# One tanh over six score banks in 12 of 56 chunks, with the VectorE work and side jobs placed anew

## The chip, the cores and the metric

The kernel runs on one core of a Trainium2 chip. The metric is the device time of one execution in microseconds (us); lower is better. Engines in the profile: PE (TensorE matmul) and PEld (its weight load), DVE (VectorE), ACT (ScalarE), POOL (GpSimd), SP (SyncE).

## The reference

Softcapped attention over 8 batches, 12 heads, 448 tokens and 64 dimensions, then a mixture of experts with soft slots over the 3584 tokens.

```python
scores = scale * np.matmul(q, k.transpose(0, 1, 3, 2))
scores = cap * np.tanh(scores / cap)                    # cap = 30
attn = np.exp(scores - max);  attn /= attn.sum(-1) + 1e-09
x = np.matmul(attn, v)                                  # -> [3584, 768]
logits = x @ phi                                        # 32 slots
d = softmax of logits over tokens;  slot_input = d.T @ x
slot_out[e] = np.maximum(slot_input[e] @ w1[e], 0) @ w2[e]   # 8 experts
out = (softmax of logits over slots) @ slot_out
```

## The kernel before

Attention works on transposed score tiles of 128 keys by 448 queries, one PSUM bank each. Four heads make a quad, each quad two pairs, each pair seven tiles: 336 tiles, sorted by `order` and cut into 56 chunks of six (`CH`). A chunk is two groups of three (`CS`). `qk_chunk(i)` (L309) writes group i into a three-bank buffer `sc` of the pool `psS` (two buffers, six banks); `tanh_chunk(i)` (L323) reads it on ScalarE into half of the SBUF tile `ex` of its chunk (five such tiles in rotation). The exp of a chunk runs in place one turn later (`exp_chunk`, L336), over the tiles that `SHARED` does not give to VectorE. VectorE computes its share (the first one to three tiles of a chunk) in seven integer and half-precision steps, numbered 0 to 6 (`poly_exp`, L560, steps at L566 to L573).

The main loop (L856) sets each engine's order by hand; there is no scheduler. One turn j issues:

- slot '0'; tanh A (`2j`); slot 'm'; tanh B (`2j+1`); slot 'e'; exp of chunk j-1;
- `pv_first` (L611): attention times V, first four tiles of the pair that ends in chunk j-2; slot 'a'; `pv_tail`;
- `qk_chunk(2j+2)`, the first scores of the next chunk; slot 'b';
- `pv_rest` (L628): the remaining three tiles, then `norm` (L595): reciprocal and multiply on VectorE (L598, L601), which frees PV's single PSUM bank for the next pair; then V casts on POOL for a later quad (L287), each followed by a load of V on SP's queue;
- slot 'c'; `qk_chunk(2j+3)`, the second scores; slot 'd'.

In the chunks with j = 6 mod 7 no pair ends, and PV is skipped.

Slots hold jobs put there by `at`: in each slot those marked '<' come first, then the plain ones, then '>'. `POLY` lists, by (turn, slot), which step of which chunk VectorE takes. `WHEN` gives the turn, relative to 7 times the batch, and the slot of the side jobs: transposes of k and q (`k1` to `q3`, L268, each with a VectorE copy at L279), V casts, loads of k and q through POOL's queue (`lk1` to `lq3`, L181), transposes of the attention output (`x0` to `x2`, L646), logits (`lg`), their exp (`ee`), slot sums (`ss`), transposes of E (`et`, L687) and their row sums (`es`, L703). These side jobs share one PSUM bank, so each waits for the copy out of the one before. `FILL` and `spare` are junk matmuls on ones. One weight load of 384 KB is issued by POOL in slot 'b' of most turns.

After the loop the tail (L887 on) finishes the last pairs, the slot sums, the two expert layers and the output.

## Time and profile before

| what | us |
|---|---|
| median of 3 runs (284.36 to 288.99) | 284.4 |
| the profiled execution | 284.53 |
| its span in the trace | 282.8 |
| PE / DVE / ACT / POOL busy | 247.6 / 241.9 / 250.7 / 139.9 |

The attention loop fills the span from about 7 to 237 us; the granted TensorE clock is 1.00 in all stages of it. A row of the page's groups gives the line, engine, operation and tile, then how many, busy us, mean ns of one, and idle time before it. A timeline row gives start, length, line, and in brackets the idle time before it with what ended it. Chunk 10's first tanh starts at 46.75 us, chunk 21's at 90.65, chunk 35's at 148.04, chunk 52's at 217.73.

### The profile page before, as it was taken

How to read it: one execution, taken by the hardware profiler on the slowest of the kernel's cores; microseconds unless marked ns; L12 is line 12 of the kernel's file. 1: busy time of each engine (PE TensorE's matmuls, PEld its weight loads, DVE VectorE, ACT ScalarE, POOL GpSimd, SP SyncE). 2: the span in 40 equal slices, each digit the busy share in tenths (PEclk: the TensorE clock that was granted, in tenths of full speed). 3: DMA queues.
4: the chain of work that ended last, by engine and by line, in shares of the span. 5: the costliest groups of instructions: out<-in, count | busy, mean ns of one | idle time of the engine just before them, and what ended most of it. 6: DMA issues, size and time to landing. Idle time of an engine off the chain costs nothing.

```text
span 282.8 us, 10259 instructions
## 1 busy us (share of the span) xinstructions
PE 247.6 (88%) x4463; PEld 164.7 (58%) x4463; DVE 241.9 (86%) x473; ACT 250.7 (89%) x211; POOL 139.9 (49%) x197
## 2 busy tenths in 40 slices
PE   8897989999999999899988998899989989998710
PEld 7555556655665667566756675667566758643300
DVE  3499999999999999999998999999999996456740
ACT  3999999999999999999999999999999996247720
POOL 7965647673957375828663758274834220200000
PEclk9999999999999999999999999999999999999975
DMA  7999999999999999999999999999999489959995
GB/s 244 261 203 205 207 214 221 231 180 219 228 225 219 219 232 232 216 216 221 227 219 211 224 216 206 217 223 216 228 215 217 106 290 331 408 209 391 412 427 247
DMA packets 58332, 68.08 MB, mean 241 GB/s; under 512 B 4144, under 2 KB 54448, under 8 KB 58288
## 3 DMA queue, kind: packets, MB, share of 16 engines
q0 software_dynamic: 42448, 35.31, 79.7%
q1 hardware_dynamic: 15552, 31.89, 32.0%
q8 instruction: 35, 0.57, 0.7%
q10 hardware_dynamic: 288, 0.23, 0.2%
q14 instruction: 9, 0.07, 0.1%
HBM read 91.72 MB, written 19.27 MB: 393 GB/s over the span
## 4 chain that ended last, share of the span: by engine, by line
DVE 40%; ACT 29%; PE 18%; issue 5%; DMA 2%; POOL 1%; DVEq 0%; ACTq 0%
ACT ex L329 16%; ACT ex L334 12%; DVE xq L601 6%; DVE ex L572 5%; DVE xp L571 4%; DVE xp L569 4%; DVE xf L568 3%; DVE ex L566 3%; DVE ex L573 3%; PE pv L591 3%; DVE qT L279 3%; DVE xT L653 2%; PE sc L320 2%; DVE xp L570 2%; DVE kT L279 2%
## 5 line engine op out<-in xcount | busy, mean ns | idle before, releaser
L329 ACT ACTIVATE ex<-sc 128x1344 f16<-128x1344 f32 (+1 forms) x113 | 154.9, 1546 | 1.2 <-PE sc L320 1.2
L334 ACT ACTIVATE ex<-ex 128x1344 bf16<-128x1344 f16 (+5 forms) x58 | 118.2, 2051 | 0.1
L591 PE MATMUL pv<-vbd,ex 128*128 128x130 bf16 (+1 forms) x1610 | 93.5, 211 | 8.9 <-DVE xq L601 4.1
L591 PEld LDWEIGHTS <-ex 128*128 128x128 bf16 (+1 forms) x1680 | 75.6, 101 | 35.4 <-PE sc L320 7.3
L287 POOL CAST vbd<-vraw 64x896 bf16<-64x896 f32 x46 | 46.7, 1016 | 62.0 <-PE pv L591 33.6
L320 PE MATMUL sc<-qT,kT 64*64 64x448 bf16 x672 | 70.6, 359 | 2.5 <-DVE qT L279 1.2
L601 DVE TENSOR_TENSOR xq<-pv,rec 128x448 bf16<-128x448 f32 x46 | 28.7, 624 | 1.6
L320 PEld LDWEIGHTS <-kT 64*64 64x64 bf16 x672 | 24.0, 105 | 10.1 <-issue 7.6
L569 DVE TENSOR_TENSOR xp<-xf 128x1344 f16<-128x1344 uint16 (+2 forms) x34 | 27.8, 817 | 0.3
L571 DVE TENSOR_TENSOR xp<-xp,xf 128x1344 f16<-128x1344 f16 (+2 forms) x34 | 26.8, 788 | 0.6
L572 DVE TENSOR_TENSOR ex<-ex,xp 128x1344 uint16<-128x1344 uint16 (+2 forms) x34 | 26.7, 787 | 0.2
L116 POOL DMA_DIRECT2D w1b<-in_moe_w_dram x32 | 25.8, 807 | 0.0
L568 DVE TENSOR_SCALAR xf<-ex 128x1344 uint16<-128x1344 uint16 (+2 forms) x34 | 18.3, 538 | 0.5
L184 POOL DMA_DIRECT2D qb<-in_q_dram x22 | 16.4, 744 | 4.2 <-PE qps L277 2.9
L570 DVE TENSOR_SCALAR xp<-xp 128x1344 f16<-128x1344 f16 (+2 forms) x34 | 17.3, 509 | 0.6
L566 DVE TENSOR_SCALAR ex<-ex 128x1344 uint16<-128x1344 f16 (+2 forms) x34 | 17.2, 506 | 0.6 <-ACT ex L329 0.6
L573 DVE TENSOR_SCALAR ex<-ex 128x1344 uint16<-128x1344 uint16 (+2 forms) x34 | 16.9, 497 | 0.3
L279 DVE COPY kT<-kps 128x896 bf16<-128x896 bf16 x23 | 14.1, 615 | 2.9 <-PE kps L274 2.8
L184 POOL DMA_DIRECT2D kb<-in_k_dram x22 | 16.3, 744 | 0.0
L120 POOL DMA_DIRECT2D w2d<-in_moe_w_dram x21 | 15.9, 769 | 0.0
L295 POOL MEMSET vbd<- 64x1 bf16 x22 | 2.8, 125 | 25.6 <-PE pv L591 25.6
L279 DVE COPY qT<-qps 128x896 bf16<-128x896 bf16 x23 | 14.2, 618 | 0.9 <-PE qps L277 0.9
(123 smaller groups left out, 305.7 us busy)
## 6 DMA issues: line engine op xcount, KB each, us to landing
w1b<-in_moe_w_dram POOLq DMA_DIRECT2D x32, 384.0 KB, 8.9
vraw<-in_v_dram SPq DMA_DIRECT2D x44, 224.0 KB, 6.0
w2d<-in_moe_w_dram POOLq DMA_DIRECT2D x21, 384.0 KB, 9.0
w2t<-w2d SPq DMA_DIRECT2D x21, 384.0 KB, 6.4
out_dram<-ob SPq DMA_DIRECT2D x7, 768.0 KB, 7.8
qb<-in_q_dram POOLq DMA_DIRECT2D x22, 224.0 KB, 7.3
kb<-in_k_dram POOLq DMA_DIRECT2D x22, 224.0 KB, 6.5
w2b<-in_moe_w_dram POOLq DMA_DIRECT2D x11, 384.0 KB, 8.0
```

The source lines that it names most:

```text
L184: pool.dma_start(out=t, in_=quad_ap(nm, Q))
L279: dve.tensor_copy(t, ps)
L287: pool.tensor_copy(vbds[Q % 2][r, :, :, c0:c0 + DH], raw[r])
L320: pe.matmul(sc[cs, u, 0:S], qkT["k", Q][r, c, cs], qkT["q", Q][r, :, cs], start=True, stop=True)
L329: act.activation(exs[j][:, half * CS + u0:half * CS + u1, :].bitcast(F16), (own[0] if i == u0 == 0 else sc)[:, u0:u1, 0:S], ACT.Tanh, scal ...
L334: act.activation(exs[j][:, u0:u1, :], exs[j][:, u0:u1, :].bitcast(F16), ACT.Exp, scale=cap)
L568: lambda: dve.tensor_scalar(s, y, STEP - 1, STEP, ALU.bitwise_and, ALU.bitwise_or),
L569: lambda: dve.tensor_tensor(p, s, s.bitcast(F16), op=ALU.mult),
L571: lambda: dve.tensor_tensor(p, p, s, op=ALU.mult),
L572: lambda: dve.tensor_tensor(y, y, p, op=ALU.add),
L591: pe.matmul(out_, exs[j][r, u, q0:q0 + (HP if tail else P)], v_, start=(c == 0 and g == gs[0] < NF), stop=(c == NT - 1), skip_group_check= ...
L601: dve.tensor_tensor(xq[Q][:, h, s0:s1, :], pv[:, 0:s1 - s0, 0:DH], rec.to_broadcast([P, s1 - s0, DH]), op=ALU.mult)
```

## The change

In the chunks of `JOINED` the two tanh become one instruction over all six banks. From chunk 10 to 52 the two `sc` buffers are one tile, the board, taken from a pool that is closed and opened anew at chunk 10 and at 53; in unjoined chunks between, waits are set by half of the board. In a joined turn the first scores of the next chunk are issued behind slot 'b' and the rest of PV. `SHARED` changes in one entry, chunk 32, from two tiles to three (93 in all). `POLY` is placed anew throughout, `FILL` and `WHEN` in part.

```diff
+    psV = attp.enter_context(tc.tile_pool(name="psV", bufs=1, space=PSUM, side="right"))
+    scp = ExitStack()
+    psS = scp.enter_context(tc.tile_pool(name="psS", bufs=2, space=PSUM))
...
+    def half_of(i):
+        nonlocal psS
+        j, half = divmod(i, CH // CS)
+        if JOINED and half == 0 and j in (JOINED[0], JOINED[-1] + 1):
+            scp.close()
+            psS = scp.enter_context(tc.tile_pool(name=f"psS{j}", bufs=2 - (j == JOINED[0]), space=PSUM,
+                                                 reuse_waits="tile"))
+            if j == JOINED[0]:
+                own["board"] = psS.tile([P, CH, 512], F32, name="sc", tag="board")
+        if JOINED and JOINED[0] <= j <= JOINED[-1]:
+            return own["board"][:, half * CS:half * CS + CS, :]
+        return psS.tile([P, CS, 512], F32, name="sc", tag="sc")
+
+    def own_half(ins, kind, i, behind=None):
+        j, half = divmod(i, CH // CS)
+        other = "qt"[kind == "q"]
+        tc.declare_no_dep(ins, group=f"{other}{1 - half}", reason="other three banks of the score buffer")
+        tc.add_to_no_dep_group(f"{kind}{half}", ins)
+        if behind is not None:
+            tc.add_manual_dep(ins, behind.name, ...)
...
     def tanh_chunk(i):
...
+        if j in JOINED:
+            if half:
+                apart["t", i - 1] = apart["t", i] = act.activation(
+                    exs[j].bitcast(F16), own["board"][:, :, 0:S], ACT.Tanh, scale=qk_scale / cap).ins
+            return
...
+    JOINED = (10, 14, 17, 21, 24, 31, 35, 38, 42, 45, 49, 52)
-    SHARED = {... 32: (2, 0), ...}
+    SHARED = {... 32: (3, 0), ...}
     POLY = {
...
-            (21, 'e'): ((21, 0),),
-            (21, '<a'): ((19, 5), (19, 6)),
+            (21, '<a'): ((19, 5), (21, 0)),
+            (21, '>a'): ((19, 6),),
...
-            (35, '0'): ((33, 6),),
-            (35, '>a'): ((35, 0),),
+            (35, 'e'): ((35, 0), (33, 6)),
...
-            (42, '>a'): ((42, 0), (40, 6)),
+            (42, 'e'): ((42, 0),),
+            (42, '<a'): ((40, 6),),
...
-    FILL = ((7, 'a', fill, 18), (6, 'b', spare, 11), (6, 'c', spare, 3),)
+    FILL = ((7, 'a', fill, 18), (6, 'a', spare, 8),)
...
-    WHEN: 'k1': (-1, 'd'), 'x1': (9, '0'), 'x2': (10, 'a'), 'et': (13, 'e'), 'es': (15, 'c'),
-          'lk1': (-3, 'd'), 'lq1': (0, 'a'), 'lk2': (1, 'c'), 'lq3': (3, 'b')
+    WHEN: 'k1': (0, '0'), 'x1': (8, 'c'), 'x2': (10, 'b'), 'et': (13, 'b'), 'es': (14, 'c'),
+          'lk1': (-2, 'm'), 'lq1': (-1, 'b'), 'lk2': (1, 'd'), 'lq3': (3, '0')
...
-        qk_chunk(2 * j + 2)
+        if j not in JOINED:
+            qk_chunk(2 * j + 2)
         run(j, "b")
...
             run(j, "r")
+        if j in JOINED:
+            qk_chunk(2 * j + 2)
         run(j, "c")
```

## The prediction

> **What bounds the kernel now.** I read the page first (busy time, slices), then the instruction groups with their shapes apart, then the timeline of ScalarE alone, then those of TensorE and VectorE around one chunk. "A" and "B" are the two tanh of a chunk, "first" and "second scores" the two groups of six score matmuls (L320) that chunk j issues for chunk j+1.

> Page, busy time and the slice row of ScalarE:

> ```profile
> PE 247.6 (88%) x4463; PEld 164.7 (58%) x4463; DVE 241.9 (86%) x473; ACT 250.7 (89%) x211; POOL 139.9 (49%) x197
> ...
> ACT  3999999999999999999999999999999996247720
> ```

> Three engines are near 88%, but only ScalarE shows nines from the second slice to the 33rd. The tail after 237 us is untouched by the change. The groups (count, busy us, mean ns):

> ```profile
> L329 ACT ACTIVATE ex<-sc 128x1344 f16<-128x1344 f32 x111 | 153.7, 1561 | 0.0
> L334 ACT ACTIVATE ex<-ex 128x2688 bf16<-128x2688 f16 x21 | 57.1, 2719 | 0.0
> L334 ACT ACTIVATE ex<-ex 128x1344 bf16<-128x1344 f16 x27 | 43.6, 1615 | 0.0
> L334 ACT ACTIVATE ex<-ex 128x1792 bf16<-128x1792 f16 x6 | 11.6, 1934 | 0.0
> ```

> These means hold overlap and are no price. ScalarE's timeline for chunks 20 and 21 (start, us; an "x2" row spans A and B):

> ```profile
> 87.10 2.76 ACT L329 ACTIVATE ex<-sc 128x1344 f16<-128x1344 f32 x2
> 89.44 1.63 ACT L334 ACTIVATE ex<-ex 128x1344 bf16<-128x1344 f16 x1
> 90.65 2.78 ACT L329 ACTIVATE ex<-sc 128x1344 f16<-128x1344 f32 x2
> 92.99 2.77 ACT L334 ACTIVATE ex<-ex 128x2688 bf16<-128x2688 f16 x1
> 95.33 2.80 ACT L329 ACTIVATE ex<-sc 128x1344 f16<-128x1344 f32 x2
> ```

> Ends (start + length) are 89.86, 91.07, 93.43, 95.76, 98.13. So end to end a tanh pair takes 2.36, exp over 1344 takes 1.21, over 2688 takes 2.33. Each starts 0.3 to 0.4 us before its forerunner ends; early on (9.31 + 2.44 = 11.75, next start 11.66) 0.09 was enough. A late start therefore costs nothing until it is later than about 0.1 before the forerunner's end. By this measure ScalarE loses nothing from 16 to 237 us: it is the bound.

> TensorE around the same chunks:

> ```profile
> 88.58 0.49 PE L696 MATMUL eps<-ident,E 128*32 128x128 bf16 x16 [0.45 <-DVE xT L653]
> 89.00 0.56 PE L320 MATMUL sc<-qT,kT 64*64 64x448 bf16 x6
> 89.50 0.66 PE L839 MATMUL junk<-ones 128*128 128x384 bf16 x3
> ...
> 90.33 0.32 PE L839 MATMUL junk<-ones 128*128 128x384 bf16 x1
> 90.58 0.57 PE L320 MATMUL sc<-qT,kT 64*64 64x448 bf16 x6
> ...
> 94.64 0.38 PE L320 MATMUL sc<-qT,kT 64*64 64x448 bf16 x2
> ```

> Second scores for chunk 21 end at 91.15, after A of 21 has started (90.65): today only B needs them. VectorE there, and the hand-over to the tail:

> ```profile
> 92.40 0.50 DVE L566 TENSOR_SCALAR ex<-ex 128x1344 uint16<-128x1344 f16 x1
> 92.81 0.85 DVE L572 TENSOR_TENSOR ex<-ex,xp 128x1344 uint16<-128x1344 uint16 x1
> 93.70 0.51 DVE L573 TENSOR_SCALAR ex<-ex 128x1344 uint16<-128x1344 uint16 x1
> ```

> ```profile
> 231.94 0.34 PE L839 MATMUL junk<-ones 128*128 128x384 bf16 x1 [0.90 <-DVE xq L601]
> ```

> In the chain that ended last ScalarE rules from 80 to 170 us; from 182 to 232 it is VectorE with short TensorE pieces, and TensorE enters the tail after waiting 0.90 for VectorE's norm.

> **The change, part by part.**

> *Twelve joins.* Exp prices: (2.33 - 1.21) / 1344 = 0.833 ns an element, fixed 1.21 - 1.12 = 0.09. A tanh of 1344: 2.36 / 2 - 1.12 = 0.06 fixed. No row shows a tanh over 2688. Low end 0 (PSUM and SBUF reads show one rate, so no loss); high end the unoverlapped start of the first tanh, 0.544 - 448 x 0.833 ns = 0.17. I take 0.06, the row of the same instruction in the same stream: 12 x 0.06 = 0.72 us saved, 0 to 2.0. [...]

> *A third tile of chunk 32 to VectorE.* Exp over 1792 ends 1.59 after its forerunner, over 1344 1.21: 0.37 saved on ScalarE. VectorE pays seven steps of 1344 for seven of 896: 4.74 - 3.78 = 0.96 us. From 140 to 160 us it is busy 18.50 of 20, so 1.5 idle covers it; uncovered, up to 0.96.

> *The joined tanh needs both score groups.* At chunks 14, 21, 42 the second scores came 0.39, 0.50, 0.61 us after A's start; past the overlap that would cost some 0.2 each; at 35 and 49 nothing. The same change moves what stands before them (junk of chunks 6 mod 7: 11 + 3 becomes 8, ahead of the first scores; the E transposes from 'e' to 'b', where they no longer wait 0.45 for the xT copy). B of chunk 20 ends 89.86; without junk in front, second scores run about 89.9 to 90.5, before 90.65. Cost 0, bound 0.7. At 10, 17, 24, 31, 38, 45 they were ready 0.17 to 0.84 before A; at 52 0.58 late, but there x1's transposes (0.75) leave the chunk ahead.

> *First scores now wait for the whole joined tanh (end E) and stand behind side jobs and the rest of PV on TensorE.* At 3 mod 7 the second scores already ran 0.05 after B's end, TensorE being ready; the first scores take that place: E + 0.05 + 0.57 + 0.04 (the shortest score-to-tanh gap shown) = E + 0.66, due at E + 1.21 - 0.1. Free by 0.4. The second scores follow as before. At 21, 35, 42 VectorE's order gets a new wait: step 0 of chunk j, which needs E, stands ahead of the last step of chunk j-2, j-2's last tile is in this PV rest, and the scores queue behind that. Chain: 0.05 + 0.42 (L566) + 0.51 (L573) + 0.43 (94.21 to 94.64) + 0.57 + 0.04 = E + 2.0, due at E + 2.33 - 0.1. It fits by 0.2. Behind step 0 on VectorE also stand that pair's norm and qT copy, and TensorE's next PV waits for the norm. Cost 0.1 in all; bound 0 to 3 x 0.5.

> *The pool is reopened at chunk 10.* The board lies over both old buffers, so the first scores of 10 wait for B of 9 (44.61) in place of A: QK starts 44.66 in place of 43.59. Second scores then end near 46.6, due 46.75. Cost 0.1, bound 1.1. At 53 the wait is for a tanh already waited for: 0.

> *Moved jobs.* Each xT group is 0.75 on TensorE and a 0.6 copy on VectorE: x1 now precedes the second scores of 1 mod 7, which had 0.8 to 1.1 to spare (0.17 at chunk 50, where e_sums' 0.33 leave and the overlap of 0.5 covers). e_sums one chunk earlier ends three waits of at most 0.4 of xps for winv. x2 passes the PV tail only; k1 passes nothing on TensorE. Loads lk1, lq1, lk2, lq3 are POOL issues of 0.74 each: lq1 goes a chunk earlier, ahead of a weight load; lq3 now stands before chunk 3 mod 7's weight load and must wait for q2's transposes just issued, some 0.5, with the V cast behind it; that cast waits for PV's end anyway (33.6 us of such waits). SP's V loads follow the casts. POOL is busy 49%. Cost 0, bound -0.5 to +0.5. Fewer junk matmuls leave TensorE idle, nothing more.

> *Sum.* ScalarE: -0.72 - 0.37 + 0.1 + 0.1 = -0.9. But the tail starts on VectorE's norm, and the chain is VectorE's from 182 on, which idles 0.7, 0.3, 0.2 in the last three stages; what is saved at chunks 45, 49, 52 (0.18) I let lapse. That leaves -0.7 to -0.8. The profiled execution took 284.53 (span 282.8 and 1.7 around it), 0.1 above the median 284.4: 283.7 against it, 283.6 against the median.

> **Rivals.**
> 1. *The full fixed cost is saved.* For: the first tanh alone shows 0.17. Against: the stream shows 0.06. 12 x 0.17 + 0.37 = 2.4: 282.0. [...]
> 2. *Given back.* VectorE, 0.96 us fuller and newly waiting for E, keeps its end at 231; or the joined tanh waits for second scores (0.7). For: it is busy 19.68 of 20 from 200 to 220. Against: 5 us idle before 182. 284.4, up to 285.3.
> 3. *Slower: scores behind PV behind VectorE.* If steps of chunk j-2 come late, the scores do, and ScalarE stops, as it never did. The longest wait of a PV weight load for L573 is 0.6. With 0.1 to 0.4 to spare, a loss of 0.2 to 0.5 in each of 12: +2.4 to +6.0 on 283.6, middle 287. Decides from 0.06 a join (gain gone); 2% from 0.5. Against: second scores sit behind the same PV rest today and arrive.
> 4. *No join in effect* (a start as late as B's): the tile remains, 284.0; part of case 2's range.

> **How the numbers follow.** Forecast 0.50; full fixed cost 0.10; given back, with 4, 0.26; slower 0.14. The forecast with its bounds runs 282.9 to 284.1; reaching to case 1's middle and through case 2 into the low part of case 3 gives 282.2 to 286.2, with under 2 in 10 outside. A change of under 2% (5.7 us) is about what a measurement of this kernel cannot tell from none. Over 2% faster 0.01; only the far end of case 3 is over 2% slower, 0.04; within 0.95.

> **What would show it.** Joined tanh rows ending about 2.30 after their forerunner, 12 of them, against 2.36; ScalarE without idle to 236; exp x1792 down to 5; second scores of chunks 13, 20, 41 ending before the joined start; first scores ending 0.65 after E at 3 mod 7 and about 2.0 at 21, 35, 42. Wrong if joined rows take 2.19 or 2.36, if ScalarE waits for L320, or if TensorE waits more than 0.90 for VectorE near 231.

## The result and the profile after

The changed kernel took 286.86 us (median of 6, 286.20 to 287.67), the kernel before 284.71 beside it on the same chip (6 runs): a ratio of 1.0077, 95% interval 1.0053 to 1.0100. It is slower by some 2.2 us, where 0.8 less than before had been forecast. The profiled execution took 286.76 with a span of 285.0 (before: 284.53 and 282.8). Every ratio here is to executions of the kernel before in the same sitting, whose median went from 284.71 to 285.76 between sittings, so times of different sittings are best compared by their ratios; executions over 1.5% slower than the fastest of their kernel count in the medians, not in the ratios.

The page of the changed kernel: busy time, ScalarE and the granted clock in 40 slices, then three groups.

```profile
PE 247.6 (87%) x4449; PEld 166.2 (58%) x4449; DVE 240.8 (84%) x473; ACT 250.5 (88%) x199; POOL 141.3 (50%) x197
...
ACT  4999988999999999999999999999999997237720
...
PEclk9999979999999999999999999999999999999975
```

```profile
L365 ACT ACTIVATE ex<-sc 128x1344 f16<-128x1344 f32 x87 | 113.6, 1402 | 1.8 <-PE sc L348 1.8
L361 ACT ACTIVATE ex<-sc 128x2688 f16<-128x2688 f32 x12 | 30.6, 2552 | 0.1
L373 ACT ACTIVATE ex<-ex 128x1792 bf16<-128x1792 f16 x5 | 9.1, 1821 | 0.0
```

ScalarE's busy time did not rise. Its row has two new eights, in slices 6 and 7 (36 to 50 us), and the clock row a new 7 in slice 6. By the idle time before them all joined tanh together waited 0.1 us; the unjoined ones 1.8, for scores. That is the prediction's sign of being wrong "if ScalarE waits for L320" (L348 in the changed kernel).

ScalarE's timeline around chunk 21 (start, length); L361 is the joined tanh:

```profile
91.55 1.44 ACT L373 ACTIVATE ex<-ex 128x1344 bf16<-128x1344 f16 x1
92.77 2.52 ACT L361 ACTIVATE ex<-sc 128x2688 f16<-128x2688 f32 x1
95.06 2.56 ACT L373 ACTIVATE ex<-ex 128x2688 bf16<-128x2688 f16 x1
```

The ends are 92.99 and 95.29: 2.30, as forecast. So the saving is there, and something else took more. I measure that as in the prediction: end of a ScalarE instruction less the end of the one before, less its usual length (tanh over 1344 1.18, over 2688 2.30; exp over 1344 1.21, and so on). What is left over is a wait. Before, all such waits from 9 us to the last exp come to 0.27; after, to 3.69:

| after, where | wait, us |
|---|---|
| chunk 8 A, chunk 8 B, chunk 9 B (38.92, 40.65, 45.06) | 0.76, 0.55, 0.84 |
| chunk 10 joined and the tanh behind it (the pool reopened) | 0.16, 0.10 |
| exp of the logits (E, 225.12) | 0.80 |
| others | 0.48 |

From the first tanh (0.41 earlier than before) to the last exp (238.95 against 237.05) the balance is -0.41 for the earlier start, -1.10 saved by the joins and the third tile, and +3.42 for more waits: +1.9. The tail added 0.3.

The largest place is chunks 8 and 9. First the waits over the whole span, after and then before, by sum, count and longest; the row of ScalarE holds one wait at the start in both (0.81 after, 1.22 before):

```profile
ACT ex L365 <- PE sc L348: 2.6, 4, 0.8
PE kps L278 <- DMA kb<-in_k_dram: 2.1, 1, 2.1
```

```profile
ACT ex L329 <- PE sc L320: 1.2, 1, 1.2
PEld L277 <- DMA kb<-in_k_dram: 1.2, 3, 0.5
```

TensorE after, then before, then ScalarE after:

```profile
32.04 0.57 PE L348 MATMUL sc<-qT,kT 64*64 64x448 bf16 x6 [0.36 <-ACT ex L365]
34.68 0.58 PE L278 MATMUL kps<-ident,kb 128*64 128x128 bf16 x14 [2.07 <-DMA kb<-in_k_dram]
...
37.95 0.93 PE L348 MATMUL sc<-qT,kT 64*64 64x448 bf16 x4
```

```profile
32.85 0.56 PE L320 MATMUL sc<-qT,kT 64*64 64x448 bf16 x6
33.48 0.58 PE L277 MATMUL kps<-ident,kb 128*64 128x128 bf16 x14
```

```profile
38.92 1.29 ACT L365 ACTIVATE ex<-sc 128x1344 f16<-128x1344 f32 x1 [0.65 <-PE sc L348]
40.65 1.29 ACT L365 ACTIVATE ex<-sc 128x1344 f16<-128x1344 f32 x1 [0.44 <-PE sc L348]
...
45.06 1.29 ACT L365 ACTIVATE ex<-sc 128x1344 f16<-128x1344 f32 x1 [0.73 <-PE sc L348]
```

The load of k for turn 7's transposes, which the scores of chunk 8 need (`lk3` of batch 0, issued by POOL), landed at 34.64 after and at 33.43 before: there 0.05 us ahead of its use. In the chain of the changed kernel that ended last it stands with its whole flight:

```profile
26.73 7.91 DMA kb<-in_k_dram
```

And the granted clock in three stretches of the changed kernel (length, then busy time of each engine, then the clock, DMA share, GB/s):

```profile
34.00:35.37 1.37, 0.69 (x17) 0.60 (x18) 0.06 (x1) 1.37 (x3) 0.00 (x0) 1.00 1.19 243
35.37:38.78 3.41, 3.24 (x44) 2.23 (x41) 3.34 (x7) 2.90 (x3) 0.00 (x0) 0.50 1.24 218
38.78:42.00 3.22, 2.52 (x48) 1.91 (x47) 2.40 (x6) 2.64 (x3) 1.65 (x2) 1.00 1.08 180
```

Behind the 2.07 us of idle TensorE its clock was halved for 3.41 us, in the very stretch in which the late transposes, PV and scores had to catch up: four score matmuls took 0.93 there (37.95), 0.54 elsewhere. Before, the clock is 1.00 from 6 to 237 us.

### The profile page after: what moved, and what is told of

It is laid out like the page before. It is cut to its first block, busy times and chain, and to the rows that moved or that the text cites. A ratio compares the mean times of both kernels' runs of the same rounds, so it can differ in the third digit from the quotient of the medians.

```text
span 285.0 us, 10218 instructions
## 1 busy us (share of the span) xinstructions
PE 247.6 (87%) x4449; PEld 166.2 (58%) x4449; DVE 240.8 (84%) x473; ACT 250.5 (88%) x199; POOL 141.3 (50%) x197
## 4 chain that ended last, share of the span: by engine, by line
ACT 45%; PE 21%; DVE 19%; DMA 5%; issue 5%; POOL 1%; DVEq 0%; ACTq 0%
ACT ex L373 19%; ACT ex L365 17%; ACT ex L361 7%; PE pv L631 3%; PE sc L348 3%; DMA kb<-in_k_dram 3%; PE so_ps L1103 2%; DVE xq L641 2%; DVE xp L609 2%; DMA out_dram<-ob 2%; DVE xp L611 2%; PE hp L1075 2%; DVE ex L612 2%; DVE xf L608 1%; DVE kT L280 1%
## 5 line engine op out<-in xcount | busy, mean ns | idle before, releaser
L365 ACT ACTIVATE ex<-sc 128x1344 f16<-128x1344 f32 (+1 forms) x89 | 114.9, 1387 | 2.6 <-PE sc L348 2.6
L373 ACT ACTIVATE ex<-ex 128x1344 bf16<-128x1344 f16 (+5 forms) x58 | 109.4, 1891 | 0.1
L631 PE MATMUL pv<-vbd,ex 128*128 128x130 bf16 (+1 forms) x1610 | 94.8, 212 | 8.0 <-DVE xq L641 3.0
L288 POOL CAST vbd<-vraw 64x896 bf16<-64x896 f32 x46 | 47.8, 1039 | 64.1 <-PE pv L631 32.8
L348 PE MATMUL sc<-qT,kT 64*64 64x448 bf16 x672 | 67.3, 361 | 2.6 <-ACT ex L365 1.2
L361 ACT ACTIVATE ex<-sc 128x2688 f16<-128x2688 f32 x12 | 30.6, 2552 | 0.1
L348 PEld LDWEIGHTS <-kT 64*64 64x64 bf16 x672 | 22.0, 105 | 8.6 <-issue 2.6
L609 DVE TENSOR_TENSOR xp<-xf 128x1344 f16<-128x1344 uint16 (+2 forms) x34 | 26.7, 786 | 0.3
L278 PEld LDWEIGHTS <-kb 128*64 128x64 bf16 x308 | 10.0, 109 | 12.4 <-issue 7.2
L278 PE MATMUL kps<-ident,kb 128*64 128x128 bf16 x308 | 12.8, 222 | 4.7 <-DVE ET L737 2.5
```

Source lines behind the costliest of these rows:

```text
L278: pe.transpose(ps[h * HP:h * HP + HP, c, :], src[:, h, c * DH:(c + 1) * DH], ident)
L288: pool.tensor_copy(vbds[Q % 2][r, :, :, c0:c0 + DH], raw[r])
L348: ins = pe.matmul(sc[cs, u, 0:S], qkT["k", Q][r, c, cs], qkT["q", Q][r, :, cs], start=True, stop=True).ins
L361: apart["t", i - 1] = apart["t", i] = act.activation(exs[j].bitcast(F16), own["board"][:, :, 0:S], ACT.Tanh, scale=qk_scale / cap).ins
L365: ins = act.activation(exs[j][:, half * CS + u0:half * CS + u1, :].bitcast(F16), (own[0] if i == u0 == 0 else sc)[:, u0:u1, 0:S], ACT.Tanh ...
L373: act.activation(exs[j][:, u0:u1, :], exs[j][:, u0:u1, :].bitcast(F16), ACT.Exp, scale=cap)
```

## The experiments

Theory 1: the late k load, behind three weight loads in POOL's queue, costs the time. Rivals: the joins themselves; the new places of x2 and VectorE's steps. Later the question became what, behind a late load, costs how much. All edits leave what is computed unchanged. "Waits" are ScalarE's, in chunks 7 to 9 unless said otherwise; each comes from the one execution of a kernel that has a trace. "Load" is the landing of that `lk3`.

**Joins alone, placement alone.**

```diff
-    JOINED = (10, 14, 17, 21, 24, 31, 35, 38, 42, 45, 49, 52)
+    JOINED = ()
```

> The changed kernel with no joined tanh at all; everything else of the change stays. Theory 1 (a late load): the k load that chunk 7's transposes wait for lands at 34.6 us, TensorE and then ScalarE stop around 38 to 46 us, and the joins have no part in it: the loss of about 2.1 us (excess over the nominal ScalarE end-to-end times in chunks 7 to 9) stays, and the whole time is within 0.7 us of the changed kernel's 286.9, so 286.2 to 287.6. Theory 2 (the joins and the reopened score pool cost): the loss goes, 284 to 285. Theory 3 (VectorE steps and side jobs placed anew in chunks 6 to 9 cost): as theory 1 in time, but the loss stays even where the load lands by 33.5.

Measured: 286.90, ratio to before 1.0071 (1.0029 to 1.0113): as slow as with joins, so the joins are not the cause. The trace is of its fastest execution, 285.37: load 34.29, waits 0.40, later ones 0.37, 0.25, 0.71.

The other way round, the kernel before with joins in 11 chunks (all but 14):

> The kernel before with the joined tanh in 11 of the 12 chunks (without 14, whose VectorE step would stand ahead of its tanh) and the score pool reopened, with the old steps, side jobs, junk and the old two tiles in chunk 32. Theory 1 and 3: joins are worth 11 x 0.06 = 0.67 us less what chunks 21, 42 and 52 lose by waiting for their second scores (about 0.2 each): 284.0 to 284.7, no stop at 38 to 46 us. Theory 2: a loss of 1.5 us or more, 286 and over.

Measured: 290.80, 1.0175 (1.0106 to 1.0244): without the new placement the joins make it slower. Where that time goes is not shown. The trace is of its slowest execution, 297.11; in it four of the 11 joined tanh waited, 0.21 to 0.30 at chunks 10, 21 and 42, and 2.53 at chunk 49, behind a halved clock (0.937 granted over that execution). Only its stretch to 60 us is used below: load 34.81, waits 1.36.

**Other loads and x2.** The first three weight loads moved from turns 1 and 2 to 8, 9 and 10:

```diff
-        at(1 + n * (NCH - 5) // len(wjobs), "b", *job)
+        at(max(2, 1 + n * (NCH - 5) // len(wjobs)) if n >= 3 else 8 + n, "b", *job)
```

> The changed kernel with its first three weight loads of 384 KB moved from turns 1 and 2 to turns 8, 9 and 10, so that 1.15 MB less stands ahead of the k load in POOL's queue (5.6 us at the 205 GB/s that this queue moves there). Theory 1: the load lands before 30 us, the stop at 38 to 46 us goes, 284.4 to 285.0. Theory 2 and 3: no change, 286.3 to 287.5.

Measured: 289.97, 1.0181 (1.0142 to 1.0220). The load landed at 32.20, there was no wait to 46 us, and the jam moved to the next quad's k, in turn 14; TensorE and ScalarE of this kernel, the latter at chunk 15:

```profile
66.73 0.96 PE L278 MATMUL kps<-ident,kb 128*64 128x128 bf16 x14 [4.24 <-DMA kb<-in_k_dram]
```

```profile
72.28 2.47 ACT L365 ACTIVATE ex<-sc 128x1344 f16<-128x1344 f32 x2 [4.91 <-PE sc L348]
```

That the weight loads ahead of it make the k load late is confirmed, at both places; as a cure it is none.

x2 back at `(10, 'a')`:

> The changed kernel with x2 back in slot 'a', ahead of the PV tail, as before. The E exp of chunk 53 ended 0.80 us late in the changed kernel's trace because its logits waited 1.0 for the xT copy. If the place of x2 is the reason, that 0.80 goes and the whole falls by up to 0.8 us (286.1); if it is VectorE's load in chunks 51 and 52, the 0.80 stays (286.9).

Measured: 287.22, 1.0050 (1.0006 to 1.0094). Load 34.52, waits 2.02, about as without the edit; the 0.80 at E was gone, and 0.50 came at 211. x2's place is no cause of the whole.

**The load earlier, the load later.** One word of `WHEN`, in both kernels:

```diff
-    'lk3': (4, 'd')
+    'lk3': (3, '0')      # early;  late: (5, 'e')
```

> The changed kernel with the loads lk3 (the k that is transposed at 7, 14, 21, ...) moved from turn 4, slot 'd', to turn 3, slot '0', ahead of two weight loads in POOL's queue. Theory 1 (the late load): it lands about 4 us or more before its transposes everywhere, the losses of about 2.1 us in chunks 8 and 9 go, 284.3 to 285.2. Theory 3 (VectorE steps and side jobs placed anew): loss stays, 286.5 to 287.5.

Measured: **284.22, 0.9955 (0.9929 to 0.9980)**: less than before, and 1.2% under the changed kernel by the two ratios. No wait at 38 to 46, the clock 1.00 to the tail, all waits 0.82 together. TensorE goes on without a gap, ScalarE too:

```profile
32.43 0.56 PE L348 MATMUL sc<-qT,kT 64*64 64x448 bf16 x6 [0.38 <-ACT ex L365]
32.93 0.58 PE L278 MATMUL kps<-ident,kb 128*64 128x128 bf16 x14
```

```profile
38.47 2.54 ACT L365 ACTIVATE ex<-sc 128x1344 f16<-128x1344 f32 x2
```

> The kernel before with the same move of lk3 alone. There the load lands 0.05 us before its transposes at chunk 7 and 0.1 to 0.2 at chunks 21 and 35. Theory 1: no loss to take away where ScalarE never waits, so no change in an undisturbed run, ratio 0.997 to 1.001, and fewer slow runs if some of its runs land late. Theory 3: no change.

Measured: 284.43, 0.9971 (0.9948 to 0.9994). By this ratio the kernel before gains a little from the early load too: its ten executions took 283.61 to 285.27, those without the edit beside them 284.12 to 289.06 (though ten more, below, had a median of 284.61). The two kernels with the early load, 284.22 and 284.43, cannot be told apart.

> The changed kernel with lk3 early and x2 back in slot 'a'. Theory 1 with x2 as the reason of the 0.8 us at chunk 53: both losses go, 283.6 to 284.6, below the kernel before. Theory 3: 286 and over.

(Early load and x2 at 'a'.) Measured: 284.46, 0.9973 (0.9947 to 0.9998).

> The kernel before itself, for a second trace. Theory 1 by chance: the first loads of quad 1 land at any time from 6.9 to 8.4 us; where they land late, its k load for chunk 7 lands late too and ScalarE loses time near 40 us. Theory 1 by the program: they land at 6.9 again. The ratio is 1 within its interval either way.

(The kernel before, run again.) Measured: 284.61, 0.9988 (0.9955 to 1.0022); its load landed at 33.92 and nothing was lost. The landing differs between executions of one order: the first raw k of the start landed between 6.9 and 8.6 us over all runs, and POOL's casts and first weight load wait for it (issued 11.19 before, 12.70 after). The trace of the kernel before, on which the prediction stands, has the earliest of these landings (6.93). With `lk3` in its place the load was issued 2.7 us ahead of chunk 6's first tanh in both orders, and took 6.29 to 8.01 us in three traces of the old order, 7.10 to 7.91 in four of the new. So it is not shown that the change itself makes the load later.

> The changed kernel with lk3 early and no joined tanh: what the joins are worth once the load is out of the way. By the ScalarE rows the twelve joins save 0.72 us and lose about 0.5 of it at chunks 10, 13, 52: this kernel is then 0.2 us slower than the one with joins (284.2), within the interval the same. If the joins' waits cost more than they save, it is faster, 283.5.

(Early load, `JOINED = ()`.) Measured: 284.59, 0.9969 (0.9945 to 0.9993). Against 284.22 the twelve joins are worth 0.37; the intervals overlap.

> The changed kernel with lk3 moved the other way, to turn 5, slot 'e', behind lk1: one issue (0.74 us) and 224 KB (1.1 us at 205 GB/s) more ahead of it, so that the k of chunk 7 lands late in every run, near 35 to 36 us. Theory 1: ScalarE's loss in chunks 7 to 10 grows with the landing, to 3 us or more, and the same load is late at chunks 21, 28, 35 too; 288 to 291.

Measured: 295.05, 1.0335 (1.0255 to 1.0415). Load 36.14, waits 3.83, and new ones of 1.8 to 2.0 at 102, 162 and 221, each behind a halving of the clock (at 96, 158 and 216); behind a fourth, at 127, three waits came to 1.4.

> The kernel before with the same late load. Theory 1 alone (only the landing counts): the same loss in chunks 7 to 10 as in the changed kernel with the late load, within 0.3 us at equal landing. Theory 1 with the new order (in the changed kernel step 6 of chunk 4 stands behind the copy of the late k on VectorE, and PV of chunk 7 waits for it): about 0.8 us less loss than there.

Measured: 291.90, 1.0224 (1.0144 to 1.0305). Load 36.21, waits 2.67. Theory 1 holds, but the changed order waits 1.2 more behind about the same landing.

**Why it pays more.** In these the load stays late in the changed kernel. VectorE's step (4, 6) ahead of the kT copy:

```diff
-            (7, '0'): ((4, 6),),
+            (7, '<0'): ((4, 6),),
```

> The changed kernel with the late load and step 6 of chunk 4 moved ahead of the k copy on VectorE at turn 7. If that order is what makes a late load dearer, the loss in chunks 7 to 10 is 0.5 to 1 us smaller than in the changed kernel with the late load, at equal landing; if only the landing counts, it is the same.

Measured: 286.82 and 295.33 in two runs; in the trace, of the slower, load 35.53, waits 4.15: not less. Then x1 back at `(9, '0')`; VectorE's steps of turns 6 to 8 as before; and both:

> Changed kernel with lk3 late at (5, e), and x1 back at (9, 0). If the place of x1 ahead of the second scores is what makes a late load dearer: the 0.83 us before B of chunk 8 falls to about 0.2, and the ScalarE waits of chunks 7 to 10 from 4.1 to about 3.4 us. If it is VectorE's order of turns 6 to 8: still about 4.1. The moved x1 changes seven later stages as well, so the total time decides nothing.

Measured: 290.78, 1.0186 (1.0055 to 1.0318). The wait before B of chunk 9 (which the expectation calls chunk 8) fell from 0.83 to 0.21, as x1's place would have it; the sum of chunks 7 to 9 did not fall (3.96). Load 36.17.

> Changed kernel with lk3 late, and VectorE's steps of turns 6 to 8 placed as in the kernel before. If VectorE's order (three steps in 7 m ahead of the kT copy) makes the late load dearer: the waits of chunks 7 to 10 fall from 4.1 to about 2.9 us. If it is x1: about 4.1, with the 0.83 before B of chunk 8 still there.

Measured: 291.61, 1.0215 (1.0072 to 1.0359); load 35.51, waits 4.07. VectorE's order alone is not it.

> Both put back, lk3 late. If these two are all of the difference, chunks 7 to 9 lose what the order before loses, 2.7 us, and with the first join (0.16 + 0.10 at chunk 10) 2.9. If k1 in (7, 0) or the joined entry bears a share, it stays above 3.2.

Measured: 289.07, 1.0126 (0.9940 to 1.0312). Load 35.13, half a microsecond later than in the changed kernel (0.2 by each trace's own chunk 7, see the table below), and the waits only 0.34. It is no cure: the clock was halved at 57.31, 152.89 and 210.91, with waits of 2.4 in chunks 12 and 13 and of 1.8 at 157 and at 216. The surprise is that the clock stayed at 1.00 up to there (rows of both put back, then of the late load alone, then of the kernel before with late load):

```profile
35.18 0.58 PE L278 MATMUL kps<-ident,kb 128*64 128x128 bf16 x14 [2.25 <-DMA kb<-in_k_dram]
```

```profile
31.00:38.00 7.00, 4.39 (x88) 2.80 (x87) 5.70 (x12) 7.00 (x6) 2.11 (x3) 1.00 1.22 232
```

```profile
31.00:38.00 7.00, 3.68 (x43) 2.20 (x39) 4.04 (x9) 6.73 (x5) 2.41 (x4) 0.77 1.22 232
38.00:46.00 8.00, 7.01 (x110) 4.63 (x107) 6.70 (x14) 5.22 (x5) 2.43 (x3) 0.77 0.73 113
```

```profile
31.00:38.00 7.00, 3.79 (x41) 2.27 (x41) 3.98 (x8) 7.00 (x5) 2.23 (x4) 0.86 1.21 231
38.00:46.00 8.00, 7.06 (x127) 4.87 (x126) 7.33 (x15) 5.66 (x6) 3.27 (x5) 0.91 0.85 134
```

The changed order with the late load was halved for 6.83 us, the old one for 3.41. So the last kernels keep the load late and TensorE busy.

**The clock kept up.** Junk matmuls ahead of chunk 7's transposes, 13 in the changed kernel, 18 in both with the late load:

```diff
+    at(6, "<d", spare, 39)        # 54 with the late load
```

> Changed kernel, and 13 junk matmuls (39 parts, some 2.1 us) ahead of chunk 7's k transposes, in batch 0 only; the load is as late as before. If the halved clock is most of the loss: clock 1.00 through 32 to 46, the ScalarE waits there fall from 2.3 to at most 0.6 us, median some 1.5 to 2 lower than the changed kernel's, 284.9 to 285.4. If the lateness itself is: the clock stays up and the waits stay near 2, median 286.9 or, as the junk can stand in front of the transposes, more.

Measured: in the trace the clock stays at 1.00 and the waits are 1.20, not the 0.6 or less expected; TensorE and stretches:

```profile
32.37 2.29 PE L881 MATMUL junk<-ones 128*128 128x384 bf16 x13
34.59 0.58 PE L278 MATMUL kps<-ident,kb 128*64 128x128 bf16 x14
...
36.31 0.34 PE L631 MATMUL pv<-vbd,ex 128*128 128x130 bf16 x3 [0.52 <-DVE ex L613]
```

```profile
31.00:38.00 7.00, 6.13 (x96) 3.64 (x97) 5.17 (x11) 7.00 (x6) 1.62 (x3) 1.00 1.23 228
```

The load landed early, at 33.67, and the transposes waited for the junk. They start 0.57 after chunk 7's first tanh, in the changed kernel 0.50, so the two can be compared. This execution, the fastest of twelve, took 284.90, but the median is 287.06, 1.0041 (1.0014 to 1.0068). That is 0.36% under the changed kernel's 1.0077, and the intervals overlap: whether most executions gained is not settled, and what they lost is not known, as only one has a trace.

> Changed kernel with lk3 late, and 18 junk matmuls (54 parts, some 2.9 us) in the same place. Halved clock: the waits of chunks 7 to 10 fall from 4.1 to about 1.5, what 1.5 us more lateness costs by itself, chunk 8's 0.83 from x1 perhaps staying. Lateness itself: still about 4. Later halvings (near 96, 127, 158, 216) are not touched by it.

Measured: 292.15 (three runs, 288.03 to 295.07), 1.0146 (1.0064 to 1.0228). In the trace, of the slowest, transposes at 36.55, clock 1.00 there, waits 3.17, of which 0.54 before B of chunk 9.

> Kernel before with lk3 late, and the same 18 junk matmuls. Halved clock: the waits of chunks 7 to 9 fall from 2.7 to about 1.2, and stand within 0.6 of those of the changed kernel with late load and junk, since the longer halving (6.83 against 3.41 us) was most of the difference between the two placements. Lateness itself: still about 2.7, and 1.4 less than the other.

Measured: 295.06 (three runs, 289.64 to 295.62). Transposes at 37.47, clock 1.00, waits 2.86, none before B of chunk 9. The first fell by 0.66, not by some 2.6 as the clock theory had said; the second rose by 0.19, with a load 1.2 later than without junk. So at full clock some 3 us of waits are left behind loads as late as these: there the lateness is the larger part.

Side by side, from the traces (us). The first tanh of an execution came at 6.08 to 6.74, so the fourth column gives the start of the transposes from chunk 7's first tanh in the same trace, and orders the rows:

| kernel | load landed | k transposes start | from chunk 7's first tanh | clock halved for, to 46 us | waits, chunks 7 to 9 |
|---|---|---|---|---|---|
| before | 33.43 | 33.48 | -1.11 | 0 | 0 |
| changed, no joins | 34.29 | 34.33 | -0.21 | 0 | 0.40 |
| before, run again | 33.92 | 33.97 | -0.09 | 0 | 0 |
| changed, x2 back | 34.52 | 34.57 | 0.40 | 3.41 | 2.02 |
| changed | 34.64 | 34.68 | 0.50 | 3.41 | 2.15 |
| changed, junk | 33.67 | 34.59 | 0.57 | 0 | 1.20 |
| before with joins | 34.81 | 34.85 | 0.59 | 3.41 | 1.36 |
| late, x1 and VectorE's steps put back | 35.13 | 35.18 | 0.68 | 0 | 0.34 |
| changed, late | 36.14 | 36.19 | 1.40 | 6.83 | 3.83 |
| late, VectorE's steps put back | 35.51 | 35.55 | 1.52 | 6.83 | 4.07 |
| before, late | 36.21 | 36.25 | 1.98 | 3.41 | 2.67 |
| late, x1 put back | 36.17 | 36.22 | 2.29 | 6.83 | 3.96 |
| changed, late, junk | 36.50 | 36.55 | 2.55 | 0 | 3.17 |
| before, late, junk | 37.43 | 37.47 | 3.19 | 0 | 2.86 |

Four rows at nearly the same lateness (0.50 to 0.68) make a square: old places at full clock 0.34, old places with the clock halved 1.36, new places at full clock 1.20, new places with the clock halved 2.15. Here "places" are those of x1 and of VectorE's steps in turns 6 to 8. So of the changed kernel's 2.15 the halved clock has 0.95 (1.02 in the old places), the new places have some 0.8, and about 0.3 is left for the lateness alone. In the 1.20, the wait before B of chunk 9, whose scores now stand behind x1, has 0.54, and PV waits 0.52 for a VectorE step that now stands behind the kT copy (36.31 above). In the changed kernel, with the clock halved, that PV wait was 0.17, which fits the miss of the edit to (4, 6). The split compares single executions and is therefore argued, not shown; the cure by the early load does not depend on it.

## Why the prediction was wrong

**The step that failed** is "Moved jobs": "Cost 0, bound -0.5 to +0.5". Its "k1 passes nothing on TensorE" is true of the order, and it counts the load issues as 0.74 of POOL each. So it priced order and issues and never asked when a load lands against when it is used. The trace of the kernel before showed that: landed 33.43, used 33.48. A margin of 0.05 behind a queue that does not pause (in the changed kernel 202 to 281 GB/s in every microsecond from 28 to 41) is a price of its own, and no rival had it. In chunks 8 and 9 the late load came to 2.15, and the early load took that away. The page's median of 6.5 us from issue to landing for such loads was in sight.

**"Fewer junk matmuls leave TensorE idle, nothing more"** failed too. Before, junk and scores kept TensorE busy to 33.4; after, it stopped at 32.61, and behind the idle stretch it had half its clock for 3.41 us, some 0.95 of the 2.15. That the missing junk was the reason is not shown: with the junk in its old place the kernel before lost its clock as well once its load was late (the rows with joins and with the late load, 3.41 each).

**x1** "precedes the second scores of 1 mod 7, which had 0.8 to 1.1 to spare": so it was, with the load in time (no wait before B of chunk 9 with the early load). Behind a late load that wait was 0.54 to 0.84 in the new place and 0.21 in the old, though moving x1 back alone did not lower the sum.

**What was right:** joined tanh end to end 2.30, twelve of them; exp over 1792 down to 5; second scores of chunk 21 ended at 92.58, before the joined start at 92.77; first scores of chunk 22 at E + 1.95 (97.24 against 95.29), forecast 2.0. At 3 mod 7 the first scores ended 0.62 to 0.63 after E in five of seven joins (forecast 0.65), and 1.09 at chunks 10 and 52. The pool's reopening cost 0.16 and 0.10 (forecast 0.1, bound 1.1). With the early load the last exp ended at 236.48 against 237.05, 0.57 of the 0.7 to 0.8 forecast; of that the span keeps 0.1 (282.7 against 282.8). These are single executions, and by time the gain over the kernel before with the same early load is 0.2, within the noise.

**The rivals.** Case 3 gave 287 as its middle (its own bounds give 287.8), near the time, but by luck: its mechanism was another, as all joined tanh waited 0.1, and the joins taken out left the time at 286.90. Case 2's wait of joined tanh for second scores falls with the same 0.1. Its other half, VectorE giving the gain back, is not decided. Case 1 falls with the 2.30.

**The 0.80 at E** was in no step. VectorE, then POOL, then ScalarE of the changed kernel, and the same VectorE step with the early load:

```profile
222.55 1.06 DVE L608 TENSOR_SCALAR xf<-ex 128x448 uint16<-128x448 uint16 x1
223.53 0.60 DVE L693 COPY xT<-xps 128x896 bf16<-128x896 bf16 x1
```

```profile
222.52 0.95 POOL L288 CAST vbd<-vraw 64x896 bf16<-64x896 f32 x1
```

```profile
225.12 0.28 ACT L718 ACTIVATE E<-lps 128x128 bf16<-128x128 f32 x1 [0.69 <-PE lps L702]
```

```profile
220.85 0.28 DVE L608 TENSOR_SCALAR xf<-ex 128x448 uint16<-128x448 uint16 x1
```

A step of 0.28 took 1.06 while POOL cast V, and the copy, the logits and E queued behind it. Before has the same collision at 230 (1.03), where ScalarE does not wait.

## What to carry to other kernels

Before moving or thinning work, list each load's landing against its first use; a margin below the spread of landings between executions (here 6.29 to 8.01 us of flight for one load against a margin of 0.05) is a cost waiting to fall due. A trace shows one landing only. An engine order that hides everything when loads are on time can be dear when one is late (at full clock, with transposes 0.57 and 0.68 after chunk 7's first tanh, the new places waited 1.20 and the old 0.34), so price it for both. Look at the granted clock behind each gap on TensorE as well: a gap of 2.07 us in the changed kernel was followed by 3.41 us at half clock, one of 2.25 us with the late load and x1 and VectorE's steps put back by none.
